# Attention in a fused kernel: other key chunks, v pooled on GpSimd, and another order at the start

## The chip, the cores and the metric

The kernel runs on one core of a Trainium2 chip. The metric is the device time of one execution in microseconds (us). The kernel before takes 1388.67 us as the median of three runs (1388.42 to 1390.24).

## The reference

Three parts run one after the other: attention with pooled keys and values, a mixture of experts with one expert per token, and a feed-forward layer. Only the first is touched:

```python
# q, k, v: (8 batches, 8 heads, 576, 64), float32
k_p = k.reshape(B, H, 72, 8, D).mean(axis=3)      # 72 pooled keys per head
v_p = v.reshape(B, H, 72, 8, D).mean(axis=3)
scores = scale * np.matmul(q, k_p.transpose(0, 1, 3, 2))
scores = scores - np.max(scores, axis=-1, keepdims=True)
attn = np.exp(scores)
attn = attn / (np.sum(attn, axis=-1, keepdims=True) + 1e-09)
return np.matmul(attn, v_p)
# then: logits = x @ w_gate + modality_bias[modality_id]; each token goes to its best expert
```

## The kernel before, in words

Attention runs over 36 tiles of 128 tokens, nine for each pair of batches. One batch has 8 heads of 72 pooled keys, 576 in all. They are held as five chunks of 128 rows: `load_kv` brings eight positions of each row, and `pool_kv` adds them up in three steps (4, 2, 1) into `kvq`, k in the left half and v in the right. Of chunks 0 to 3 each spans two heads, from rows 0, 160, 288 and 448; chunk 4 gathers 32 rows of 128 to 159 and 96 rows of 416 to 511.

A batch is prepared by `prep` or `kv_t` (three transposes by TensorE for each half `z` of the heads, six in all; the keys go scaled into `bd`, the values into `vT`) and by `prep2` (products of v with the gate weights, `pw`; GpSimd multiplies v by masks `mk` into `vb`, so that a chunk has a column block for each head in it, zero outside that head).

A tile goes through six stages. `stage_q` transposes q (four), `stage_s` multiplies with `bd` and takes the maximum on VectorE, `stage_x0` and `stage_e` are the exponentials on ScalarE, `stage_t` transposes `e` (five) and ScalarE copies `eT`, and `stage_a` multiplies `eT` with `vb` into `u` (the attention output, its gate logits and the row sum, 73 columns per head). VectorE and ScalarE (`stage_x`) divide by the row sum, four heads each. Scores of tiles 0 and 1 of a batch (half of the heads each) are both needed for `e` of either.

The order on TensorE, VectorE, ScalarE and SyncE's queue is the order of the code; on GpSimd the scheduler sets it. In pass `i` of the loop the code runs `stage_t(i)`, `stage_e(i+2)`, `stage_x`, `stage_q(i+4)`, `stage_s(i+3)`, what the tables `sched` have for that tile, and `stage_a(i)`. VectorE also gets routing operations between its own (`run_fill`). In front of the loop the first tiles are written out by hand. A PSUM pool `ps_s` has three banks, and `ps_t`, `ps_q` and each half of `u` one.

## Time and profile before

| | us |
|---|---|
| median of three runs | 1388.67 |
| profiled execution | 1387.1 |
| its span in the profile | 1385.3 |
| PE busy | 1357.2 (98%) |
| VectorE busy | 929.2 (67%) |
| ScalarE busy | 641.8 (46%) |
| GpSimd busy | 157.1 (11%) |
| attention's last product with v starts | 179.00 |

Times in the profile count from the start of the span. TensorE has two rows: PEld loads weights, PE multiplies, and loads overlap products. A product on float32 shows two loads and two products in the profile (x12 for six products), a transpose one. The time from the first load of one group to the first load of the next is what the group took on TensorE, waits included.

### The profile page before, as it was taken

Reading aid. Unit: us, or ns where it says so; the run is one execution under the profiler, and the core shown is the slowest. Engines: PE = TensorE matmul, PEld = TensorE weight load, DVE = VectorE, ACT = ScalarE, POOL = GpSimd, SP = SyncE. Lnnn points to the kernel's source line nnn. Section 1 sums busy time; section 2 is a strip of 40 time slices with the busy share of each in tenths; the row PEclk is TensorE's granted clock in tenths of the full one; section 3 lists DMA queues with packets and bytes.
Section 4 is the critical chain, followed back from the end, with each engine's and each line's share of the span. In section 5 each row is a group of like instructions: output and inputs, shape, how many; then the busy total and the mean of one; then the engine's idle time right before and its main releaser. Section 6 shows DMA issues by size and latency. Waiting matters only on the chain.

```text
span 1385.3 us, 24324 instructions
## 1 busy us (share of the span) xinstructions
PE 1357.2 (98%) x7658; PEld 1257.9 (91%) x7658; DVE 929.2 (67%) x1883; ACT 641.8 (46%) x1403; POOL 157.1 (11%) x188
## 2 busy tenths in 40 slices
PE   7999999999999999999999999999999999999998
PEld 5888889999999999999888888888889888888987
DVE  6988776888888888887786445644644564565443
ACT  4888854554455545454444324433433342343322
POOL 3243331111101111100001000100000010001001
PEclk9999999999999999999999999999999999999999
DMA  9996367878778777766645544644454455445441
GB/s 282 291 315 205 119 204 227 262 240 247 238 239 244 239 218 219 218 215 204 193 136 154 167 121 115 178 149 119 123 177 145 116 161 164 115 122 161 120 115 69
DMA packets 229815, 254.41 MB, mean 184 GB/s; under 512 B 19288, under 2 KB 191868, under 8 KB 229724
## 3 DMA queue, kind: packets, MB, share of 16 engines
q1 hardware_dynamic: 223964, 233.16, 56.8%
q0 software_dynamic: 5760, 20.10, 4.0%
q8 instruction: 50, 0.82, 0.3%
q14 instruction: 41, 0.34, 0.1%
HBM read 206.74 MB, written 46.47 MB: 183 GB/s over the span
## 4 chain that ended last, share of the span: by engine, by line
issue 56%; PE 3%; POOL 2%; DVE 1%; DMA 0%; ACT 0%; POOLq 0%; DVEq 0%; ACTq 0%
POOL out_dram L1108 2%; PE ph L943 2%; PE y L956 1%; DVE wl L786 0%; DMA ws<-in_moe_w_dram 0%; ACT wh L785 0%; DVE lo L948 0%; PE pt L871 0%; POOLq L1356 0%; DVE dm L799 0%; DVE da L797 0%; DVE wo L809 0%; ACT hi L947 0%; POOLq L1108 0%; DVE dex L798 0%
## 5 line engine op out<-in xcount | busy, mean ns | idle before, releaser
L1129 PE MATMUL hps<-yc,sq 128*128 128x384 f32 x2004 | 404.3, 336 | 0.6
L1129 PEld LDWEIGHTS hps<-yc,sq 128*128 128x128 f32 x2004 | 358.6, 188 | 32.7 <-ACT s L1170 2.6
L1119 PE MATMUL ops<-wo,gh 128*128 128x512 f32 x1152 | 358.5, 392 | 0.0
L1119 PEld LDWEIGHTS ops<-wo,gh 128*128 128x128 f32 x1152 | 211.4, 188 | 23.1
L1119 PE MATMUL ops<-wo,gl 128*128 128x512 f32 x576 | 228.7, 397 | 0.0
L1141 ACT ACTIVATE r<-c,three 128x384 f32<-128x384 f32 x144 | 88.9, 617 | 205.8 <-DVE c L1151 205.4
L1145 ACT CAST gh<-r 128x384 fp32r<-128x384 f32 x192 | 98.6, 514 | 130.0 <-DVE r L1142 128.6
L786 DVE TENSOR_TENSOR wl<-ws,wh 128x512 fp32r<-128x512 f32 x192 | 129.5, 711 | 15.2 <-ACT wh L785 14.5
L785 ACT CAST wh<-ws 128x512 fp32r<-128x512 f32 x192 | 113.3, 620 | 53.5 <-DMA ws<-in_moe_w_dram 42.1
L956 PE MATMUL y<-hi,wh 128*128 128x400 f32 x384 | 135.0, 351 | 0.5 <-ACT hi L947 0.5
L956 PE MATMUL y<-lo,wh 128*128 128x400 f32 x384 | 132.6, 345 | 1.3 <-DVE lo L948 1.1
L943 PE MATMUL ph<-xhi,wh 128*128 128x400 f32 x384 | 131.9, 344 | 1.0 <-PEq L1356 0.8
L943 PE MATMUL ph<-xlo,wh 128*128 128x400 f32 x384 | 132.7, 345 | 0.0
L943 PE MATMUL ph<-xhi,wl 128*128 128x400 f32 x384 | 132.6, 345 | 0.0
L956 PE MATMUL y<-hi,wl 128*128 128x400 f32 x384 | 131.5, 342 | 0.0
L1119 PEld LDWEIGHTS ops<-wo,gl 128*128 128x128 f32 x576 | 107.9, 187 | 23.1
L1146 DVE TENSOR_TENSOR gl<-r,gh 128x384 fp32r<-128x384 f32 x192 | 106.5, 555 | 31.7 <-ACT gh L1145 27.0
L1108 POOL DMA_INDIRECT out_dram<-osb,tki x36 | 35.3, 979 | 771.9 <-ACT osb L1106 740.7
L1142 DVE SCALAR_TENSOR_TENSOR r<-r,c 128x384 f32<-128x384 f32 x144 | 80.3, 558 | 54.5 <-ACT r L1141 52.4
L863 POOL TENSOR_TENSOR cxg<-cxg 100x512 f32<-100x512 f32 x48 | 57.2, 1194 | 335.6 <-PE ph L943 206.2
L1142 DVE SCALAR_TENSOR_TENSOR r<-r,hps 128x384 f32<-128x384 f32 x48 | 26.6, 554 | 98.3 <-ACT r L1141 98.2
L1141 ACT ACTIVATE r<-hps,three 128x384 f32<-128x384 f32 x48 | 27.9, 582 | 132.1 <-PE hps L1129 132.0
(222 smaller groups left out, 1907.0 us busy)
## 6 DMA issues: line engine op xcount, KB each, us to landing
sq<-sd SPq DMA_DIRECT2D x336, 256.0 KB
ws<-in_moe_w_dram SPq DMA_DIRECT2D x192, 256.0 KB, 3.8
sd<-wq SPq DMA_DIRECT2D x16, 896.0 KB
cxg<-xr SPq DMA_DIRECT2D x44, 225.8 KB
yr<-yd SPq DMA_DIRECT2D x12, 768.0 KB
cs<-in_moe_w_in_dram SPq DMA_DIRECT2D x34, 256.0 KB, 3.7
kv<-in_k_dram SPq DMA_DIRECT2D x16, 512.0 KB
kv<-in_v_dram SPq DMA_DIRECT2D x16, 512.0 KB
```

Of the source, the lines that this page charges most:

```text
L785: nc.scalar.copy(hi, src)
L786: nc.vector.tensor_tensor(lo, src, hi.bitcast(F32), op=ALU.subtract)
L863: nc.gpsimd.tensor_tensor(s.xg[:, t, 0:DM].rearrange("p (h x) -> p h x", x=D), v, s.xg[:, t, GC:GC + 1].unsqueeze(2).to_broadcast([T4, H, ...
L943: nc.tensor.matmul(ph, a[j][:, 0, k * P:(k + 1) * P], b[k], start=(n == 0), stop=(n == 11))
L956: nc.tensor.matmul(yps[d], a[j][:, 1, d * P:(d + 1) * P], b, start=(f == 0 and n == 0), stop=(f == 7 and n == 2))
L1108: i_ = nc.gpsimd.indirect_dma_start(out=out, out_offset=bass.IndirectOffsetOnAxis(ap=tki[:, c:c + 1], axis=0), in_=o, in_offset=None).ins
L1119: nc.tensor.matmul(pso[t_], gt[a][:, t * P:(t + 1) * P], wo[f][:, b], start=(q == 0 and fh == th and n == 0), stop=(q == NQ - 1 and fh != ...
L1129: nc.tensor.matmul(ps, w[:, kk, a * P:(a + 1) * P], y[:, b, kk], start=(start and n == 0), stop=(n == 5), skip_group_check=True)
L1141: a_.activation(r, c, AF.Relu, bias=g.three)
L1142: v.scalar_tensor_tensor(r, r, 6.0, c, op0=ALU.min, op1=ALU.mult)
L1145: a_.copy(gh, r)
L1146: late.append(lambda: v.tensor_tensor(gl, r, gh.bitcast(F32), op=ALU.subtract))
```

## The change

The chunks are five plain runs of 128 rows, from rows 0, 256, 360, 448 and 128 (`KS`), so heads are split into 5 and 3 (`ZH`). Chunk 4 covers three heads, the others two (`HD`). `prep` makes three transposes for the first half and two for the second. `stage_a` opens each half with a product over all of its heads (chunk 4 into five heads, chunk 2 into three; `vb` has zero column blocks for that) and adds the others. `prep2` multiplies by the gate weights in three products that contract over 128 rows instead of six over 64. `stage_e` is one activation instead of two.

GpSimd (`p_`) pools v of batches 0 and 1; VectorE (`v_`) did so before. At the start the tiles go 0, 1, 2 instead of 0, 2, 1; `stage_t(1)` moves in front of the transposes of v of batch 0; and k of batch 1 is pooled behind `prep2(0)`.

```diff
-KR = (0, 160, 288, 448)
+KS = (0, 256, 360, 448, 128)
+HD = ((0, 2), (3, 2), (5, 2), (6, 2), (1, 3))
+VB = (5, 7, 9, 12, 1)
+NB = 14
+ZC = ((4, 0, 1), (2, 3))
+ZH = ((0, 5), (5, 3))
...
-                rows = bass.AP(tensor=src.tensor, offset=src.offset + 288 * z * x, ap=[[x, P], [160 * x, 2], [1, x]])
+                rows = bass.AP(tensor=src.tensor, offset=src.offset + KS[2 * z] * x, ap=[[x, P], [(KS[2 * z + 1] - KS[2 * z]) * x, 2], [1, x]])
                 nc.sync.dma_start(t[:, 2 * z:2 * z + 2], rows)
             else:
-                nc.sync.dma_start(t[0:32, 4], src[128:160])
-                nc.sync.dma_start(t[32:128, 4], src[416:512])
+                nc.sync.dma_start(t[:, 4], src[KS[4]:KS[4] + P])
...
+    def kv_tz(b, d1, ps, z):
+        for c in ZC[z]:
+            o = KS[c] - KS[2 * z]
+            nc.tensor.transpose(ps[0:d1, o:o + P], kvq[b][:, c, 0:d1], g.idn)
...
+    def put_k(b, ps, z, e0):
+        h, n = ZH[z]
+        k8 = ps[0:64, 0:SP * n].rearrange("p (h k) -> p h k", k=SP)
+        if e0:
+            nc.vector.tensor_scalar(bd[b % 3][64:128, h:h + n, SP:2 * SP], k8, KSC, None, op0=ALU.mult)
+        else:
+            nc.scalar.activation(bd[b % 3][64:128, h:h + n, SP:2 * SP], k8, AF.Copy, scale=KSC)
+        nc.scalar.activation(bd[b % 3][0:64, h:h + n, 0:SP], k8, AF.Copy, scale=KSC)
+
+    def put_v(b, ps, z):
+        if z == 0:
+            nc.scalar.copy(vTs[b % 2][0:64, 0:3 * P], ps[64:128, 0:3 * P])
+        else:
+            a = ps[64:128, 0:P]
+            a = bass.AP(tensor=a.tensor, offset=a.offset, ap=[a.ap[0], [KS[3] - KS[2], 2], [1, P]])
+            nc.scalar.copy(vTs[b % 2][64:128, 0:2 * P].rearrange("p (c x) -> p c x", c=2), a)
...
         pw = ps_s.tile([P, 512], F32, name="pw", tag="s")
-        v3 = vT.rearrange("p (z x) -> p z x", z=2)
-        for c in range(4):
-            nc.tensor.matmul(pw[:, 64 * c:64 * c + 64], vT[64:128, KR[c]:KR[c] + P], wg[64:128, :], start=True, stop=True)
-        for z in range(2):
-            nc.tensor.matmul(pw[32 * z:32 * z + 32, 256:320], v3[64:128, z, P:160], wg[64:128, :], start=True, stop=True)
+        two = lambda t, o, d, n: bass.AP(tensor=t.tensor, offset=t.offset + o * E, ap=[t.ap[0], [d * E, 2], [1, n * E]])
+        nc.tensor.matmul(two(pw, 1, 9, 4), vT[:, P:2 * P], two(wg, 1, 3, 4), start=True, stop=True)
+        nc.tensor.matmul(two(pw, 5, 4, 3), vT[:, 0:P], two(wg, 0, 5, 3), start=True, stop=True)
+        nc.tensor.matmul(pw[:, 7 * E:9 * E], vT[:, 2 * P:3 * P], wg[:, 3 * E:5 * E], start=True, stop=True)
...
         t = vb[b % 3]
...
+        for c, o, n, d in ((0, 5, 2, 2), (2, 9, 2, 3), (4, 1, 3, 0)):
+            m = 1 if c == 4 else 2
+            tv = bass.AP(tensor=t.tensor, offset=t.offset + o * UX, ap=[t.ap[0], [d * UX, m], [UX, n], [1, D]])
+            tm = bass.AP(tensor=mk.tensor, offset=mk.offset + o, ap=[mk.ap[0], [d, m], [1, n]])
+            sh = [P, m, n, D]
+            nc.gpsimd.tensor_tensor(tv, x[:, c:c + m, D:2 * D].unsqueeze(2).to_broadcast(sh), tm.unsqueeze(3).to_broadcast(sh), op=ALU.mult)
+        nc.vector.tensor_tensor(t[:, 1:NB, D:XE], pw[:, E:NB * E].rearrange("p (j e) -> p j e", e=E),
+                                mk[:, 1:NB].unsqueeze(2).to_broadcast([P, NB - 1, E]), op=ALU.mult)
...
         if t < 4:
-            h = t % 2
-            i4 = bass.AP(tensor=d.tensor, offset=d.offset, ap=[d.ap[0], [144, 2], [88, 2], [1, 56]])
-            nc.scalar.activation(e[:, :, 136 + 256 * h:248 + 256 * h].rearrange("p a (c x) -> p a c x", c=2), i4, AF.Exp)
-            nc.scalar.activation(e[:, :, 32 * h:32 * h + 32], d[:, 0].rearrange("p (a x) -> p a x", a=2)[:, :, 56:88], AF.Exp)
+            c = 4 * SP * (t % 2) + SP
+            nc.scalar.activation(e[:, :, c:c + 2 * SP], d[:, 0].rearrange("p (t x) -> p t x", t=2), AF.Exp)
         else:
-            i4 = bass.AP(tensor=d.tensor, offset=d.offset, ap=[d.ap[0], [288, 2], [160, 2], [1, P]])
-            nc.scalar.activation(e[:, 0, 64:].rearrange("p (a c x) -> p a c x", a=2, c=2), i4, AF.Exp)
-            nc.scalar.activation(e[:, 0, 0:64].rearrange("p (a x) -> p a x", a=2), d[:, :, P:160], AF.Exp)
+            nc.scalar.activation(e[:, 0], d.rearrange("p x k -> p (x k)"), AF.Exp)
...
-            c0 = 64 + c * P if c < 4 else 0
-            nc.tensor.transpose(ps[:, c * P:(c + 1) * P], e[:, c0:c0 + P], g.idn)
...
         for z in range(2):
-            for n, (c, j, h) in enumerate(((2 * z, 4 * z, 0), (2 * z + 1, 4 * z + 2, 2), (4, 8 + 2 * z, 1))):
+            for n, c in enumerate(ZC[z]):
+                h, m = HD[c] if n else ZH[z]
+                h -= ZH[z][0]
+                v0 = VB[c] - (c == 4)
                 for b, p0, p1 in halves(i):
-                    nc.tensor.matmul(u[z][p0:p1, h:h + 2].rearrange("p j x -> p (j x)"), o[:, c, p0:p1],
-                                     vb[b % 3][:, j:j + 2].rearrange("p j x -> p (j x)"), start=n == 0, stop=n == 2)
+                    nc.tensor.matmul(u[z][p0:p1, h:h + m].rearrange("p j x -> p (j x)"), o[:, c, p0:p1],
+                                     vb[b % 3][:, v0:v0 + m].rearrange("p j x -> p (j x)"), start=n == 0, stop=n == len(ZC[z]) - 1)
...
         x, u, rs = xo.pop(0)
         for c in range(4):
-            nc.scalar.activation(x[:, 4 + c], u[:, c, 0:XE], AF.Copy, scale=rs[:, 4 + c:5 + c])
+            nc.scalar.activation(x[:, 4 + c], u[1][:, c - 1, 0:XE] if c else u[0][:, 4, 0:XE], AF.Copy, scale=rs[:, 4 + c:5 + c])
...
+    for c0, c1_ in ((0, 2), (4, 5), (2, 4)):
+        pool_kv(0, 1, p_, c0, c1_)
     pool_kv(0, 0, v_, 0, 2)
     pool_kv(0, 0, v_, 4, 5)
     ps = kv_ps()
     kv_t(0, D, ps, (0,))
-    put_k(0, ps, (0,))
+    put_k(0, ps[:, 0:512], 0, True)
     stage_q(0)
     pool_kv(0, 0, v_, 2, 4)
     stage_s(0)
     stage_x0(0)
+    kv_t(0, D, ps, (1,))
+    put_k(0, ps[:, 512:1024], 1, True)
+    stage_q(1)
+    stage_s(1)
+    stage_x0(1)
     stage_q(2)
-    kv_t(0, D, ps, (1,))
-    put_k(0, ps, (1,))
+    stage_e(0)
+    stage_e(1)
     stage_s(2)
     stage_x0(2)
-    stage_q(1)
-    pool_kv(0, 1, v_, 0, 2)
-    pool_kv(0, 1, v_, 4, 5)
-    pool_kv(0, 1, v_, 2, 4)
-    stage_s(1)
-    stage_x0(1)
-    stage_e(0)
-    prep_v(0)
-    stage_e(1)
     stage_q(3)
-    pool_kv(1, 0, v_, 0, 2)
-    pool_kv(1, 0, v_, 4, 5)
-    pool_kv(1, 0, v_, 2, 4)
-    prep2(0)
-    at2(1, lambda: pool_kv(1, 1, v_, rs=(2, 1)))
+    for c0, c1_ in ((0, 2), (4, 5), (2, 4)):
+        pool_kv(1, 1, p_, c0, c1_)
     at2(3, bias_all)
     at2(1, lambda: unit_consts(tc, g, c1))
...
-        stage_t(i)
-        stage_e(i + 2)
+        if i != 1:
+            stage_t(i)
+            stage_e(i + 2)
...
+        if i == 0:
+            stage_t(1)
+            stage_e(3)
+            for z in range(2):
+                prep(0, z, "v")
+            prep2(0)
+            for c0, c1_ in ((0, 2), (4, 5), (2, 4)):
+                pool_kv(1, 0, v_, c0, c1_)
         for fn_ in sched2.get(i, ()):
             fn_()
         fill.extend(route_b())
         stage_a(i)
         if i == 0:
-            pool_kv(1, 1, v_, rs=(4,))
             for z in range(2):
                 prep(1, z, "k")
             stage_q(4)
```

On TensorE, from the transposes of v of batch 0 on (`kvps`), through the first transposes of e (`tps`) to the second product with v (`ups`; `qps` are the transposes of q, `sps` the scores), the kernel before has:

```order
L179 MATMUL kvps<-idn,kvq 128x128 x6
L250 MATMUL qps<-idn,q 128x128 x4
L222 MATMUL pw<-wg,vT 128x64 x4
L224 MATMUL pw<-wg,vT 32x64 x2
L323 MATMUL tps<-idn,e 128x128 x5
L280 MATMUL sps<-bd_133,qT 128x144 x4
L344 MATMUL ups<-vb_130,eT 128x146 x6
L204 MATMUL kvps<-idn,kvq 64x128 x6
```

and the kernel after, over the same stretch, from the transposes of q of tile 3:

```order
L255 MATMUL qps<-idn,q 128x128 x4
L323 MATMUL tps<-idn,e 128x128 x5
L285 MATMUL sps<-bd_136,qT 128x144 x4
L323 MATMUL tps<-idn,e 128x128 x5
L191 MATMUL kvps<-idn,kvq 128x128 x5
L230 MATMUL pw<-wg,vT_139 128x2x32
L231 MATMUL pw<-wg,vT_139 128x2x24
L232 MATMUL pw<-wg,vT_139 128x16
L347 MATMUL ups<-vb_133,eT 128x365
L347 MATMUL ups<-vb_133,eT 128x146 x2
L347 MATMUL ups<-vb_133,eT 128x219
L347 MATMUL ups<-vb_133,eT 128x146
```

Both first transposes of e now stand in front of the transposes of v, and a tile's product with v has 1022 columns in five products where it had 876 in six.

On VectorE, from the pooling of v of batch 0 (`kvq<-kv`) on to the gate products of batch 0, the kernel before has (`kv` rows are the first two steps of a pooling):

```order
L173 TENSOR_TENSOR kvq<-kv 128x2x64
L286 TENSOR_REDUCE mx<-sps 128x4 x2
L291 TENSOR_TENSOR d<-sps,mx 128x2x2x72
L173 TENSOR_TENSOR kv<-kv 128x2x256
L173 TENSOR_TENSOR kv<-kv 128x2x128
L173 TENSOR_TENSOR kvq<-kv 128x2x64
L173 TENSOR_TENSOR kv<-kv 128x256
L173 TENSOR_TENSOR kv<-kv 128x128
L173 TENSOR_TENSOR kvq<-kv 128x64
L173 TENSOR_TENSOR kv<-kv 128x2x256
L173 TENSOR_TENSOR kv<-kv 128x2x128
L173 TENSOR_TENSOR kvq<-kv 128x2x64
```

and the kernel after, from the scores of tile 3 to the first row sums (`rs`):

```order
L291 TENSOR_REDUCE mx<-sps 128x4 x2
L296 TENSOR_TENSOR d<-sps,mx 128x2x2x72
L240 TENSOR_TENSOR vb_133<-pw,mk 128x13x8
L186 TENSOR_TENSOR kv<-kv 128x2x256
L186 TENSOR_TENSOR kv<-kv 128x2x128
L186 TENSOR_TENSOR kvq<-kv 128x2x64
L186 TENSOR_TENSOR kv<-kv 128x256
L186 TENSOR_TENSOR kv<-kv 128x128
L186 TENSOR_TENSOR kvq<-kv 128x64
L186 TENSOR_TENSOR kv<-kv 128x2x256
L186 TENSOR_TENSOR kv<-kv 128x2x128
L186 TENSOR_TENSOR kvq<-kv 128x2x64
```

The nine pooling operations that VectorE keeps at the start are those of k of batch 1, and they stand behind the gate products of batch 0 (`vb<-pw`), where before they stood in front of them.

## Rows read from the trace of the kernel before

**Rows 1.** Page: busy time by engine; a group of the last stage (busy, mean | idle).
```profile
PE 1357.2 (98%) x7658; PEld 1257.9 (91%) x7658; DVE 929.2 (67%) x1883; ACT 641.8 (46%) x1403; POOL 157.1 (11%) x188
...
L1119 PE MATMUL ops<-wo,gh 128*128 128x512 f32 x1152 | 358.5, 392 | 0.0
```

**Rows 2.** Timeline of PEld, end of attention: start, us, line, out<-in, count.
```profile
179.00 1.55 PEld L344 LDWEIGHTS ups<-vb,eT 128*128 128x128 f32 x12
```

**Rows 3.** Windows: busy of PE, PEld, DVE, ACT, POOL; PEclk, DMA share, GB/s.
```profile
10.00:20.00 10.00, 7.28 (x43) 6.05 (x42) 7.76 (x19) 3.48 (x12) 1.90 (x5) 0.83 1.07 331
20.00:30.00 10.00, 8.24 (x56) 7.59 (x54) 7.66 (x21) 6.55 (x21) 0.62 (x1) 0.83 0.98 247
110.00:120.00 10.00, 10.00 (x84) 9.53 (x84) 8.39 (x23) 8.82 (x32) 5.46 (x5) 1.00 1.06 295
120.00:130.00 10.00, 8.43 (x95) 7.75 (x94) 9.30 (x36) 8.69 (x27) 1.61 (x2) 1.00 0.44 160
```

**Rows 4.** Timeline of PEld, 149 to 156 us.
```profile
149.11 0.37 PEld L204 LDWEIGHTS kvps<-idn,kvq 128*128 128x128 f32 x3
149.45 1.55 PEld L344 LDWEIGHTS ups<-vb,eT 128*128 128x128 f32 x12
150.93 0.59 PEld L323 LDWEIGHTS tps<-idn,e 128*128 128x128 f32 x5
...
153.11 0.96 PEld L222 LDWEIGHTS pw<-wg,vT 64*128 64x128 f32 x8
154.14 0.14 PEld L224 LDWEIGHTS pw<-wg,vT 64*32 64x32 f32 x4
154.37 1.54 PEld L344 LDWEIGHTS ups<-vb,eT 128*128 128x128 f32 x12
```

**Rows 5.** Timeline of PEld, two waits; in brackets the wait and its releaser.
```profile
47.00 1.54 PEld L344 LDWEIGHTS ups<-vb,eT 128*128 128x128 f32 x12 [1.48 <-issue]
...
145.52 0.10 PEld L428 LDWEIGHTS <-tri 128*128 128x128 bf16 x1 [1.48 <-DVE d L291]
```

**Rows 6.** Timeline of PEld, first and third scores.
```profile
9.66 1.57 PEld L280 LDWEIGHTS sps<-bd,qT 128*128 128x128 f32 x8 [1.33 <-ACT qT L252]
...
16.05 1.03 PEld L280 LDWEIGHTS sps<-bd,qT 128*128 128x128 f32 x8 [1.33 <-ACT qT L252]
```

**Rows 7.** Timeline, start of attention, VectorE.
```profile
15.43 1.14 DVE L173 TENSOR_TENSOR kv<-kv 128x512 f32<-128x512 f32 x2
...
20.64 1.14 DVE L173 TENSOR_TENSOR kv<-kv 128x512 f32<-128x512 f32 x2
...
24.12 0.29 DVE L173 TENSOR_TENSOR kvq<-kv 128x128 f32<-128x128 f32 x1
```

**Rows 8.** Timeline of PEld from the fourth scores to those of batch 1.
```profile
23.76 1.99 PEld L280 LDWEIGHTS sps<-bd,qT 128*128 128x128 f32 x8
25.65 2.29 PEld L344 LDWEIGHTS ups<-vb,eT 128*128 128x128 f32 x12
...
30.70 0.42 PEld L250 LDWEIGHTS qps<-idn,q 128*128 128x128 f32 x4 [1.14 <-ACT qT L252]
31.09 1.04 PEld L280 LDWEIGHTS sps<-bd,qT 128*128 128x128 f32 x8
```

**Rows 9.** What the pooling on VectorE (line 173) waited for: us, times.
```profile
  DMA kv<-in_k_dram: 3.5, 1
```

**Rows 10.** Timeline of VectorE and GpSimd, both on two SBUF inputs, 42 to 50 us.
```profile
42.25 0.68 POOL L492 TENSOR_TENSOR t<-mf,bb 128x288 f32<-128x288 f32 x1
...
42.36 1.25 DVE L173 TENSOR_TENSOR kv<-kv 128x640 f32<-128x640 f32 x1
43.00 1.26 POOL L493 TENSOR_TENSOR bia<-bia,t 128x288 f32<-128x288 f32 x1
...
48.09 0.81 DVE L173 TENSOR_TENSOR kv<-kv 128x640 f32<-128x640 f32 x1
...
49.51 1.04 POOL L229 TENSOR_TENSOR vb<-kvq,mk 128x512 f32<-128x512 f32 x1 [5.24 <-DVE rs L352]
```

More of the change, by code (lines that the diff above doesn't have):

```diff
@@ L100, in attention @@
     nc.vector.memset(zb, 0.0)
[L101 to L102 removed]
+    wg = c1.tile([P, H * E], F32, name="wg")
+    nc.vector.memset(wg, 0.0)
+    mk = c1.tile([P, NB], F32, name="mk")
     nc.gpsimd.memset(mk, 1.0)
[L104 to L111 removed]
+    for n in (0, 4, 11):
+        nc.gpsimd.memset(mk[:, n:n + 1], 0.0)
+    for n in range(5):
+        for r in range(HD[n][1]):
+            m = mk[:, VB[n] + r:VB[n] + r + 1]
+            h = HD[n][0] + r
+            lo, hi = max(SP * h - KS[n], 0, 40 if n == 3 else 0), min(SP * (h + 1) - KS[n], P)
+            if lo > 0:
+                nc.gpsimd.affine_select(m, m, pattern=[[0, 1]], compare_op=ALU.is_ge, fill=0.0, base=-lo, channel_multiplier=1)
+            if hi < P:
+                nc.gpsimd.affine_select(m, m, pattern=[[0, 1]], compare_op=ALU.is_ge, fill=0.0, base=hi - 1, channel_multiplier=-1)
+    vb = [c1.tile([P, NB, UX], F32, name=f"vb{i}") for i in range(3)]
     bd = [c1.tile([P, H, 2 * SP], F32, name=f"bd{i}") for i in range(3)]
+    vTs = [c1.tile([P, 3 * P], F32, name=f"vT{i}") for i in range(2)]
     nc.gpsimd.memset(bd[0], 0.0)
+    for i in range(2):
+        nc.gpsimd.memset(vTs[i][64:128, 2 * P:3 * P], 0.0)
     for i in range(3):
[L115 removed]
+        for n in (0, 4, 11):
+            nc.gpsimd.memset(vb[i][:, n, 0:XE], 0.0)
         nc.scalar.activation(vb[i][:, :, XE:UX], mk.unsqueeze(2), AF.Copy, scale=float(POOL))
@@ L203, in prep @@
-        for c, o in ((4, P - 32 * z), (2 * z, 0), (2 * z + 1, 160)):
-            nc.tensor.transpose(ps[0:d1, o:o + P], kvq[b][:, c, 0:d1], g.idn)
+        kv_tz(b, 2 * D if "v" in which else D, ps, z)
         if "k" in which:
-            k8 = ps[0:64, 0:288].rearrange("p (h k) -> p h k", k=SP)
-            nc.scalar.activation(bd[b % 3][64:128, 4 * z:4 * z + 4, SP:2 * SP], k8, AF.Copy, scale=KSC)
-            nc.scalar.activation(bd[b % 3][0:64, 4 * z:4 * z + 4, 0:SP], k8, AF.Copy, scale=KSC)
+            put_k(b, ps, z, False)
@@ L350, in stage_a @@
         rs = p3.tile([P, H], F32, name="rs", tag="rs")
-        for z in range(2):
-            nc.vector.tensor_scalar(rs[:, 4 * z:4 * z + 4], u[z][:, :, XE], POOL * 1e-9, None, op0=ALU.add)
+        for z, (h, m) in enumerate(ZH):
+            nc.vector.tensor_scalar(rs[:, h:h + m], u[z][:, :, XE], POOL * 1e-9, None, op0=ALU.add)
             run_fill()
@@ L517, in attention @@
     load_kv(0, 1, (0, 2, 1))
-    nc.sync.dma_start(wg[64:128].rearrange("p (h e) -> p h e", e=E), wgh)
+    for z, (h, n) in enumerate(ZH):
+        nc.sync.dma_start(wg[64 * z:64 * z + 64, E * h:E * (h + n)].rearrange("p (h e) -> p h e", e=E), wgh[:, h:h + n])
     load_kv(1, 0, (0, 2, 1))
```

58 lines of the change are left out of this document (9 added, 49 removed).

## The prediction

> **What bounds the kernel now.** I read the page first: PE is busy for 98% of the span, VectorE for 67%, and in the last stage PE stands idle for 0.0 us before the products of the costliest groups [rows 1]. Nothing of that stage is changed, so it passes on whatever attention gains or loses. The timeline of the weight loads shows where attention ends: its last product with v starts at 179.00 [rows 2], and the first expert's products follow without a pause. What counts is therefore how much later or earlier that moment comes. (PE stands for TensorE, z for one half of the heads, k1 for k of batch 1.)
>
> Next the windows, by stage. At 110 to 120 us PE is busy for 10.00 of 10 us and VectorE for 8.39; at 120 to 130 it is 8.43 against 9.30 [rows 3]. So PE sets the pace most of the time, and in between there are stretches in which it waits for VectorE. The loads' timeline shows such waits one by one: 1.48 us at 47.00 ("issue", behind VectorE's and ScalarE's work on the previous output), and 1.48 us at 145.52 for VectorE's `d` [rows 5]. In the first 30 us no engine is full: PE has 7.28 and 8.24 of 10, at a mean granted clock of 0.83, and VectorE 7.76 and 7.66 [rows 3]. There it is a chain from engine to engine.
>
> **The change part by part.**
>
> *Product with v.* From 149.45 to 150.93 one tile's six products, 876 columns, took 1.48 us on PE [rows 4], 1.69 ns per column. They now have 365 + 146 + 146 + 219 + 146 = 1022 columns, 146 more, so 0.247 us more. The transposes beside them need 0.11 us each, so weight loads of this shape keep pace with the columns, and one load fewer gives nothing. Over 36 tiles: +8.9 us of PE time. Below this nothing speaks for a gain, except that the loads were the limit after all: five products for six would then give 1.48/6 = 0.25 us less per tile.
>
> *Transposes of k and v.* Three took 149.45 - 149.11 = 0.34 us [rows 4]; one of six goes, 0.11 us for each of 8 batches: -0.9 us.
>
> *Gate products.* Eight loads of 128 columns took 154.14 - 153.11 = 1.03 us, 0.129 each, though a product has only 64 columns; with the four small ones it is 1.26 us [rows 4]. Now there are three products, six loads: 6 x 0.129 = 0.77 us. That is -0.49 us a batch, -3.9 us in all. If the wider contraction made loads slower it would be less; were columns the limit (128 instead of 384), up to -0.8 us a batch.
>
> Together PE has 8.9 - 0.9 - 3.9 = +4.1 us more. Not all of it lies on the path: a wait for VectorE takes up what was added since the last one. Going through the loads from 45 to 170 us, from the wait at 47.00 to the one at 145.52 and two smaller ones behind it [rows 5], I find about 12 tiles out of 29 with a wait over 0.4 us. I take 40% of growth and savings alike as covered: 0.6 x 4.1 = +2.4 us. The ends are 0 (all covered) and +4.1 (none).
>
> *Exponentials, masks, row sums.* One activation instead of two, one VectorE operation instead of two per batch, and the first head of ScalarE's four now comes from the other half of `u`. ScalarE is busy for 8.82 and 8.69 of 10 us [rows 3], VectorE was treated above; I cost this at nothing. What hides it is PE's own time. Without that cover it could give back some 0.1 us a tile in the waiting tiles, 1 us, or cost as much, since the first product of a tile now waits for ScalarE's first output too, where only the second half did.
>
> *The start.* Scores of the first and the third tile start at 9.66 and 16.05 [rows 6], 3.2 us a tile, before the pooling of v (from 15.43 [rows 7]) gets in the way. At this pace the fourth comes at 19 to 20 instead of 23.76 [rows 8]. But before the first product with v PE now also has the second tile's transposes, and ScalarE the copies behind them: about 1.2 us for the fourth scores, then some 3 us on ScalarE (four exponentials, `eT`, `e`, two `vT`), then gate products and masks, 1 us. The product comes at about 25.4, against 25.65 [rows 8]: no gain there by itself.
>
> Then the pooling of k1 decides. Before, VectorE did it from 20.64 to 24.41 [rows 7], 3.77 us, in the shadow of other work; the scores of batch 1 followed at 31.09 [rows 8]. Now it stands behind `vb<-pw` in VectorE's order, so it starts at about 25.4 and ends at 29.2 at the earliest. Behind it wait the two last transposes of k1 (0.3), two copies into `bd` (0.8), `qT` (0.6), the next transposes of q, which wait for `qT` as at 30.70 [rows 8] (0.4), and then the scores: 31.5, so +0.4 us. Row sums and the first outputs are queued behind the pooling on VectorE, and ScalarE's outputs wait for them, but they are due only after those scores.
>
> *v on GpSimd.* VectorE is rid of some 4 us for each of two batches. But GpSimd works at the same time as that pooling. k0, q0, v0, k1 and q1 (6.0 MB) lie in front of v1 in the queue; at 331 GB/s [rows 3] v1 arrives from 21 or 22 us on. A GpSimd operation on 512 columns takes 1.04 us [rows 10]; scaled to the smaller steps, v1 needs about 5.4 us, and 1.7 us more for the masks, till 29. The trace shows what two such operations do to each other: on 640 columns VectorE needs 0.81 us alone and 1.25 beside GpSimd, which needs 0.68 alone and 1.26 beside VectorE [rows 10]. With 0.44/0.81 = 54% on three quarters of the 3.77 us (the rest are gaps between dependent steps) the pooling of k1 takes 1.5 us longer. The start: 0.4 + 1.5 = +1.9 us. The ends: -1.5 us, if the fourth scores come at 19 and ScalarE is quicker than I add up, and +2.9 us, if every step waits for GpSimd. Pooling of v0 is done by about 19, before PE comes to it at 22. SyncE's queue issues one DMA less per load; the loads of batches 2 and 3 wait for buffers that are pooled some 7 us later than before. That is hidden as long as pooling doesn't wait for data: it did so once, 3.5 us at the very start [rows 9].
>
> [...]
>
> **Sum.** +2.4 (tiles) + 1.9 (start) = +4.3 us. Against its own time the profiled execution of 1387.1 us becomes 1391.4; the median of the runs is 1388.67, 1.6 us above it, so 1393.0.
>
> **The rivals.**
>
> *Covered (no change).* ScalarE and VectorE, at 8.4 to 9.3 of 10 us [rows 3], are near enough to full that they set the tile's pace and PE's growth disappears in its waits; the start comes out even. For it: the waits in [rows 5]. Against it: 10.00 of 10 us of PE at 110 to 120 [rows 3], and a load timeline without gaps from 149.45 to 150.93 [rows 4]. It gives 0 to +2 us, 1389.7.
>
> *Faster.* The start is what the edit gives: the fourth scores move from 23.8 to 19 and VectorE loses the pooling of v. If the first product with v starts 3 us earlier, at 22.5, and GpSimd is through with its steps on v1 by then (or they hardly meet), batch 1's scores come at 28.5, 2.6 us earlier. With nearly all of PE's growth covered, and 1 us from ScalarE's single exponential, that is -3.5 us: 1385.2. It decides if those scores start before 28. Against it: ScalarE's list of seven operations behind the fourth scores.
>
> *More than the sum.* All of the growth on the path (+4.1), every step of k1's pooling behind GpSimd (+2.9), and a low clock after it: after the waits of the first 20 us PE's mean clock fell to 0.83 [rows 3], and the first product with v took 2.29 us instead of 1.55 [rows 8, 4]. A second idle time from 27 to 33 us could bring this once more, +1.5 us: +8.5, 1397.2.
>
> **How the numbers follow.** Forecast 0.55, covered 0.20, faster 0.10, more 0.15. The range of 8 in 10 goes from 1386.5, which cuts off most of the faster case, to 1397.0. A difference under 0.2% (2.8 us) can't be told from none in such a kernel. Of the forecast's 0.55 I give 0.08 to an outcome under +2.8; with the covered case "same" is 0.28, "faster" 0.10, and "slower" 0.47 + 0.15 = 0.62.
>
> **What would show it.** In the new profile one tile's product with v should take 1.7 us between loads, the gate products 0.75 to 0.8 us, and pooling steps of k1 on VectorE should be drawn out beside GpSimd's on v1, with batch 1's first scores at 32 to 34 us. The last product with v should start at 182 to 185 instead of 179.00. I am wrong if the product with v doesn't grow, if those scores come before 30, or if the waits at `d` shrink by as much as the products grow.

## The result, and the profile after

The changed kernel takes 1397.78 us (median of 6 runs, 1396.10 to 1398.84), the kernel before on the same occasion 1388.60 (6 runs, 1387.76 to 1390.24): a ratio of 1.0064, 95% interval 1.0053 to 1.0075. That is 9.2 us slower. The forecast had 4.3 us and a range up to 1397.0, so the direction was right and the size wrong.

TensorE's busy time on the page of the profile after, which answers to [rows 1], grew by 4.5 us:

```profile
PE 1361.7 (98%) x7520; PEld 1254.9 (90%) x7520; DVE 925.9 (66%) x1864; ACT 638.8 (46%) x1368; POOL 168.0 (12%) x224
```

Where the time went is read from three moments on the loads' timeline: the third tile's transposes of `e` (the end of the start), the last product with v, and the first expert product.

| profiled execution | third tile's transposes | last product with v | first expert product |
|---|---|---|---|
| before | 33.55 | 179.00 | 180.68 |
| after | 39.67 | 187.74 | 189.67 |
| difference | +6.1 | +8.7 | +9.0 |

So the start cost 6.1 us, the tiles 2.6, and the passage into the experts 0.3. (The spans of these two executions differ by 10.5 us, 1395.8 against 1385.3; the other 1.5 lie behind the first expert product, where nothing was changed.) These are the rows of after for the second and the third column, which answer to [rows 2]:

```profile
187.74 1.79 PEld L347 LDWEIGHTS ups<-vb,eT 128*128 128x128 f32 x10
...
189.67 0.19 PEld L950 LDWEIGHTS ph<-xhi,wh 128*128 128x128 f32 x1
```

The windows show the start. They answer to [rows 3], with 30 to 40 us added (PE, PEld, DVE, ACT, POOL; PEclk, DMA share, GB/s):

```profile
10.00:20.00 10.00, 7.19 (x46) 6.37 (x46) 4.49 (x10) 5.91 (x20) 8.62 (x21) 0.88 1.08 365
20.00:30.00 10.00, 6.04 (x35) 4.68 (x33) 6.62 (x11) 3.06 (x9) 8.71 (x13) 0.80 0.88 227
30.00:40.00 10.00, 8.08 (x32) 6.78 (x31) 3.61 (x11) 4.60 (x14) 1.11 (x2) 0.51 1.06 380
110.00:120.00 10.00, 9.28 (x76) 8.57 (x74) 8.17 (x26) 9.07 (x29) 2.00 (x2) 1.00 0.84 252
```

GpSimd is now busy for 8.6 and 8.7 of 10 us, VectorE is relieved from 10 to 20 us, and from 30 to 40 us PE has a mean granted clock of 0.51, and 0.50 in each window of 2 us from 28 to 38. The timeline of the weight loads shows how it got there; it answers to [rows 8]:

```profile
21.83 0.20 PEld L191 LDWEIGHTS kvps<-idn,kvq 128*128 128x128 f32 x2 [0.50 <-issue]
23.63 0.30 PEld L230 LDWEIGHTS pw<-wg,vT 128*128 128x128 f32 x2 [1.60 <-ACT vT L215]
...
24.90 2.33 PEld L347 LDWEIGHTS ups<-vb,eT 128*128 128x128 f32 x10 [0.53 <-DVE vb L240]
29.44 0.40 PEld L191 LDWEIGHTS kvps<-idn,kvq 128*64 128x64 f32 x3 [2.21 <-issue]
31.45 0.18 PEld L191 LDWEIGHTS kvps<-idn,kvq 128*64 128x64 f32 x2 [1.62 <-issue]
31.67 0.87 PEld L255 LDWEIGHTS qps<-idn,q 128*128 128x128 f32 x4
33.67 0.72 PEld L255 LDWEIGHTS qps<-idn,q 128*128 128x128 f32 x4 [1.13 <-ACT qT L257]
34.37 1.99 PEld L285 LDWEIGHTS sps<-bd,qT 128*128 128x128 f32 x8
36.27 0.58 PEld L347 LDWEIGHTS ups<-vb,eT 128*128 128x128 f32 x2
...
39.67 0.63 PEld L323 LDWEIGHTS tps<-idn,e 128*128 128x128 f32 x5
```

The first product with v comes at 24.90, 0.75 us earlier than before. While it runs, at about 26, the clock falls: the window from 24 to 28 us has a mean of 0.76, the one from 30 to 40 above 0.51. (The higher clock is 1.00, as from 110 to 120 us, the lower one 0.50.) Before that PE had waited 0.50, 1.60 and 0.53 us with work in between. At the lower clock it then waits 2.21 and 1.62 us for k1, the scores of batch 1 come at 34.37 instead of 31.09, and still at the lower clock they take 36.27 - 34.37 = 1.90 us and the product with v behind them 39.67 - 36.27 = 3.40 us; at the higher clock these are 0.97 and 1.72 (rows of a later tile below). This is the first of these windows:

```profile
24.00:28.00 4.00, 3.16 (x15) 2.42 (x14) 3.35 (x5) 0.00 (x0) 3.84 (x5) 0.76 0.57 144
```

What PE waited for is on VectorE, which answers to [rows 7]:

```profile
24.77 2.11 DVE L186 TENSOR_TENSOR kv<-kv 128x512 f32<-128x512 f32 x2
26.91 0.70 DVE L186 TENSOR_TENSOR kvq<-kv 128x128 f32<-128x128 f32 x1
...
30.86 0.48 DVE L186 TENSOR_TENSOR kvq<-kv 128x128 f32<-128x128 f32 x1
```

and beside it on GpSimd:

```profile
24.87 3.32 POOL L186 TENSOR_TENSOR kv<-kv 128x512 f32<-128x512 f32 x3
...
29.78 0.76 POOL L186 TENSOR_TENSOR kvq<-kv 128x64 f32<-128x64 f32 x1
```

The pooling of k1 runs from 24.77 to 31.34, 6.57 us instead of 3.77; its first two steps took 2.11 us, where before they took 1.14 [rows 7]. GpSimd's pooling of v1, and its masks, lie beside it all the while.

The steady state, where one tile follows the other, answers to [rows 4]:

```profile
156.78 0.26 PEld L191 LDWEIGHTS kvps<-idn,kvq 128*128 128x128 f32 x2
157.05 1.78 PEld L347 LDWEIGHTS ups<-vb,eT 128*128 128x128 f32 x10
158.77 0.59 PEld L323 LDWEIGHTS tps<-idn,e 128*128 128x128 f32 x5
159.33 0.47 PEld L255 LDWEIGHTS qps<-idn,q 128*128 128x128 f32 x4
159.77 1.04 PEld L285 LDWEIGHTS sps<-bd,qT 128*128 128x128 f32 x8
160.74 0.31 PEld L230 LDWEIGHTS pw<-wg,vT 128*128 128x128 f32 x2
160.97 0.30 PEld L231 LDWEIGHTS pw<-wg,vT 128*128 128x128 f32 x2
161.19 0.30 PEld L232 LDWEIGHTS pw<-wg,vT 128*128 128x128 f32 x2
161.42 1.79 PEld L347 LDWEIGHTS ups<-vb,eT 128*128 128x128 f32 x10
```

A product with v takes 158.77 - 157.05 = 1.72 us (forecast 1.7), the gate products 161.42 - 160.74 = 0.68 (forecast 0.77), scores 0.97.

### The profile page after: what moved, and what is told of

Its sections match the earlier page's. It is cut to its first block, busy times and chain, and to the rows that moved or that the text cites. A ratio compares the mean times of both kernels' runs of the same rounds, so it can differ in the third digit from the quotient of the medians.

```text
span 1395.8 us, 24016 instructions
## 1 busy us (share of the span) xinstructions
PE 1361.7 (98%) x7520; PEld 1254.9 (90%) x7520; DVE 925.9 (66%) x1864; ACT 638.8 (46%) x1368; POOL 168.0 (12%) x224
## 4 chain that ended last, share of the span: by engine, by line
issue 56%; PE 2%; POOL 2%; DVE 1%; DMA 0%; ACT 0%; POOLq 0%; SPq 0%; DVEq 0%; ACTq 0%
POOL out_dram L1115 2%; PE y L963 1%; PE ph L950 1%; DMA ws<-in_moe_w_dram 0%; DVE wl L793 0%; DVE lo L955 0%; ACT wh L792 0%; PE pt L878 0%; DVE wo L816 0%; POOLq L1363 0%; DVE dex L815 0%; ACT dex L801 0%; DVE da L804 0%; DVE dm L806 0%; DVE yo L907 0%
## 5 line engine op out<-in xcount | busy, mean ns | idle before, releaser
L1126 PEld LDWEIGHTS ops<-wo,gh 128*128 128x128 f32 x1152 | 211.4, 188 | 23.1
L1126 PEld LDWEIGHTS ops<-wo,gl 128*128 128x128 f32 x576 | 107.9, 187 | 23.1
```

The costliest lines, as they stand in the source:

```text
L1126: nc.tensor.matmul(pso[t_], gt[a][:, t * P:(t + 1) * P], wo[f][:, b], start=(q == 0 and fh == th and n == 0), stop=(q == NQ - 1 and fh != ...
```

## The experiments

The kernels were timed on four occasions, each beside the kernel before (ratio to it with 95% interval). On the first three the kernel before itself took 1400.6 to 1401.0 us, on the fourth 1388.3. The expectations of the first occasion (`e1` to `e4`) name times as if it took 1388.6; they are read as differences from that.

### The parts apart

**Chunks alone** (`e4_chunks`): the changed kernel with the start of before.

```diff
-    for c0, c1_ in ((0, 2), (4, 5), (2, 4)):
-        pool_kv(0, 1, p_, c0, c1_)
     pool_kv(0, 0, v_, 0, 2)
...
+    pool_kv(0, 1, v_, 0, 2)      # and 4:5, 2:4; tiles 0, 2, 1 again
...
-        if i != 1:
-            stage_t(i)
-            stage_e(i + 2)
+        stage_t(i)
+        stage_e(i + 2)
```

> The new chunks alone: the kernel after with the start of the kernel before (v pooled by VectorE, tiles 0, 2, 1, k of batch 1 pooled in front of the gate products). Theory (start): only the tiles' part is left, 2.0 us between the third and the last tiles and 0.9 at the end: 1390.5 to 1392. Rival (columns): 1395 to 1397.

Measured: 1.0039 (1.0025 to 1.0053), +5.4 us, more than expected. In its trace the third tile's transposes come at 35.30, so 1.75 us were lost at the start even in the old order, where TensorE was slow from 23.1 to 28 us at least, by its loads (its scores at 25.29 took 1.90 us, at the higher clock 0.97; in before the clock was 0.50 from 23.7 to 27.2); the rest, some 3.6 us, agrees with the tiles' +2.6 within the interval (3.5 to 7.4 for the whole).

**Start alone** (`e5_start`): the kernel before with the new start.

```diff
+    for c0, c1_ in ((0, 2), (4, 5), (2, 4)):
+        pool_kv(0, 1, p_, c0, c1_)
...
+        pool_kv(1, 1, p_, c0, c1_)
...
+        if i == 0:
+            stage_t(1)
+            stage_e(3)
...
+                pool_kv(1, 0, v_, c0, c1_)
```

> The start of the changed kernel (GpSimd adds up v of both batches, e's transposes of tile 1 ahead of those of v) on the old chunks. Theory (the start carries two thirds: 6.1 us at the first tile's transposes, from the shared additions of k and v and from the low clock behind them): 4.5 to 6.5 us above the kernel before, k1's additions on VectorE 6 to 7 us long, the clock at 0.50 for some 10 us, an AV stage still 1.48 us. Rival (the chunks carry it, and the start's delay is made up in waits later): at most 3 us above.

Measured: 1.0026 (1.0015 to 1.0038), +3.6 us, between the two. The transposes come at 38.90, 5.4 us later than before, so part of the delay may be made up later; where stays open, since the pauses told of in the last section lie between. The pooling of k1 took 6.26 us in its trace, beside GpSimd. The two parts, 5.4 + 3.6 = 9.0 us, make up the whole, each of them good to about 2 us.

**The changed kernel again**, on the second and the third occasion (`c_after`, `g_after`).

> The changed kernel itself again, beside the three runs below on one chip. Theory (start and columns, nothing of the chip): 1.0064 times the kernel before, its last transposes of the first tile near 39.7 us and the first expert product 9 us later than in the kernel before. Rival (some of the +9.2 was that chip's own): a ratio under 1.005. It also shows whether the common pauses of 1.9 to 2.1 us of all engines after 100 us, which the first four kernels showed and neither the kernel before nor the changed one did, belong to the chip (then they are here too) or to those kernels (then they are not).

> The changed kernel once more, so that the next run is compared with it on one and the same chip. Both theories: 1.006 times the kernel before.

Measured: 1.0060 (1.0047 to 1.0074) and 1.0058 (1.0046 to 1.0070). Transposes at 40.09 and 39.20, so the end of the start in a single trace is good to about half a microsecond. The slow stretches vary more: in `c_after` the scores at 9.70 and 34.88 took 1.84 and 1.90 us (0.97 at the higher clock), and the loads of the product with v at 25.26 took 2.43 instead of 1.79, much as in after; in `g_after` the granted clock is 0.50 only from 31.3, behind a wait of 2.82 us, to 38.2, though the scores at 10.04 took 1.85 us there too, in windows that have it at 1.00.

### What makes the start late

**k1 earlier** (`e1_k1_first`): pooling of k1 on VectorE ahead of `vb<-pw`.

```diff
     stage_q(3)
+    pool_kv(1, 0, v_, 0, 2)
...
             stage_e(3)
+            pool_kv(1, 0, v_, 4, 5)
+            pool_kv(1, 0, v_, 2, 4)
...
-            for c0, c1_ in ((0, 2), (4, 5), (2, 4)):
-                pool_kv(1, 0, v_, c0, c1_)
```

> The kernel after, with the pooling of k of batch 1 moved in VectorE's order in front of the gate products of batch 0 (its first chunks in front of the fourth tile's maximum). Theory (start): of the 9.2 us lost, 6.1 arise before the second tile's output, because this pooling stands behind the gate products, runs beside GpSimd and leaves PE idle until its clock is low. Then batch 1's first scores come at 31 to 32 us instead of 34.4, at the full clock, and the time is 1391.5 to 1393.5. Rival (columns): the wider products with v cost nearly all of it and the start is made up for later; then 1397 to 1398.

Measured: 1.0063 (1.0050 to 1.0075); nothing gained. The steps met GpSimd all the same, only earlier, and now stood in front of `vb`: one of them took 1.25 us (0.29 in before), and `vb` came at 29.05 instead of 24.58. Some 2.4 us of that, by the author's estimate, are a slow TensorE: the first three scores took 1.84 to 1.85 us each here, 0.97 at the higher clock (so they did in the next run, whose `vb` came at 27.00); some 2 us are left for the steps. VectorE's timeline of this run:

```profile
22.24 1.25 DVE L186 TENSOR_TENSOR kvq<-kv 128x128 f32<-128x128 f32 x1
...
29.05 0.26 DVE L240 TENSOR_TENSOR vb<-pw,mk 128x104 f32<-128x104 f32 x1
```

**v1 on VectorE** (`e2_v1_vector`):

```diff
-    for c0, c1_ in ((0, 2), (4, 5), (2, 4)):
-        pool_kv(1, 1, p_, c0, c1_)
+    at2(1, lambda: pool_kv(1, 1, v_, rs=(2, 1)))
...
         if i == 0:
+            pool_kv(1, 1, v_, rs=(4,))
```

> The kernel after, but v of batch 1 is pooled by VectorE, at the places of the kernel before; GpSimd pools only v of batch 0. Theory (start, by contention): the pooling of k of batch 1 takes 3.8 us instead of 6.6, batch 1's scores come at about 31.6, and the time is 1392.5 to 1395; VectorE has 2.8 us of pooling more, which its pauses hide. Rival (place alone): the pooling's place behind the gate products is what costs, beside GpSimd or not: 1396.5 to 1398. Rival (columns): 1397 to 1398.5.

The contention is gone, as its timeline of VectorE shows: 27.18 to 30.95, 3.77 us again, and 1.14 for the steps that took 2.11 in after.

```profile
27.18 1.14 DVE L186 TENSOR_TENSOR kv<-kv 128x512 f32<-128x512 f32 x2
28.35 0.29 DVE L186 TENSOR_TENSOR kvq<-kv 128x128 f32<-128x128 f32 x1
...
29.48 1.14 DVE L186 TENSOR_TENSOR kv<-kv 128x512 f32<-128x512 f32 x2
30.66 0.29 DVE L186 TENSOR_TENSOR kvq<-kv 128x128 f32<-128x128 f32 x1
```

```profile
35.83 0.59 PEld L323 LDWEIGHTS tps<-idn,e 128*128 128x128 f32 x5
```

The transposes come at 35.83, 4.88 us behind the end of the pooling (after: 8.33). But in this trace PE was slow up to nearly 22 us (the first three scores in 1.84 to 1.85 us each instead of 0.97, the last of them from 17.99), all of it came 2.4 us later (first product with v at 27.32, in after at 24.90), and the time hardly moved: 1.0052 (1.0036 to 1.0068).

**Clock in the late gaps** (`e3_warm`): ten products of zeros where PE waits for k1.

```diff
+            idle = ps_q.tile([P, 512], F32, name="wps", tag="q")
             for z in range(2):
+                for _ in range(4 - z):
+                    nc.tensor.matmul(idle, zb[:, 0:P], zb[:, 0:512], start=True, stop=True)
                 prep(1, z, "k")
             stage_q(4)
+            # and three more into a tile of ps_t
```

> The kernel after, with ten products of zeros that nobody reads in PE's idle time between the first product with v and batch 1's scores (four, three and three). Theory (clock): the low clock from 26 to 39.6 us costs some 3 us on the scores and the second product with v; with PE busy the clock is back before the scores, the second product with v takes 1.7 instead of 3.4 us, and the time is 1394.5 to 1396. Without a cost of the clock: 1397.5 to 1399, since the products of zeros only add work.

```profile
36.38 0.59 PEld L323 LDWEIGHTS tps<-idn,e 128*128 128x128 f32 x5
```

From 14 us on every scores group up to the third tile's transposes takes 0.96 or 0.97 us, as at the higher clock. The pooling of k1 still takes some 6.55 us beside GpSimd and ends at about 31.50, estimated from the loads on either side of it (the product with v at 25.09, the last transposes of k1 at 31.62; in after 24.90 and 31.45), but the transposes of `e` come at 36.38, again some 4.9 us behind it and 3.3 us earlier than in after; the time again doesn't show it, 1.0063 (1.0050 to 1.0075). The two single edits left open whether the start reaches the end at all.

**Both** (`e11_start_eased`): the edits of the two runs above together.

> The changed kernel, with both terms of its start that were sized too small taken away: VectorE adds up v of batch 1 as before (no shared additions of k1 and v1), and ten products of zeros stand in TensorE's gaps of the start (its clock has no idle time to fall in). Theory (these two are the 4 us by which the start exceeded the forecast, and they reach the end): the first tile's transposes near 35 us instead of 40, and 3.5 to 5 us less than the changed kernel in the same call. Rival (what the start gains is lost again in waits later, as the ends of the two single edits suggest, 7.5 and 8.2 us above the kernel before): within 1 us of the changed kernel.

Measured: 1.0035 (1.0023 to 1.0047) against 1.0058 (1.0046 to 1.0070) for the changed kernel on the same occasion, 1406.39 against 1408.97: 2.6 us less, good to about 2, and short of the 3.5 expected. Transposes at 37.52, not 35: again at the lower clock (0.50) from 8 to 21.6 us, and once more from 28.4 to 31.8.

**Clock in all gaps** (`e13_start_full`): the same, with products of zeros in the early gaps too, into the bank of `u` that is not in use yet (`warm(n)` issues n of them).

```diff
-    for _ in range(WU):
+    for _ in range(WU + 6):
...
+    warm(6)
     stage_s(0)
...
+    warm(6)
     stage_s(1)
...
+    warm(5)
     stage_s(2)
```

> The changed kernel with its start eased altogether: batch 1's v on VectorE as before, and products of zeros in every gap of TensorE up to the third tile (before the first scores too, where the run with products in the late gaps alone still fell to 0.50). Theory (contention and the clock are all by which the start was late beyond its place): clock 1.00 from 6 us on, third tile's transposes at 33.5 to 35 us, and what is left over the kernel before is the growth of the products with v: 2 to 3.5 us. Rival (the start does not reach the end, or something else in it is late): transposes after 36, or 5 us and more over the kernel before.

Windows of this run, and the end of the start on the loads' timeline:

```profile
8.00:24.00 16.00, 12.40 (x90) 9.83 (x88) 7.77 (x17) 9.89 (x30) 10.85 (x32) 1.00 1.11 350
24.00:28.00 4.00, 3.66 (x12) 2.88 (x13) 3.77 (x12) 0.00 (x0) 0.00 (x0) 0.59 0.20 18
28.00:40.00 12.00, 11.74 (x92) 9.75 (x92) 9.12 (x22) 8.83 (x28) 1.65 (x3) 1.00 1.05 376
```

```profile
31.63 1.04 PEld L285 LDWEIGHTS sps<-bd,qT 128*128 128x128 f32 x8
32.59 1.80 PEld L347 LDWEIGHTS ups<-vb,eT 128*128 128x128 f32 x10
34.33 0.59 PEld L323 LDWEIGHTS tps<-idn,e 128*128 128x128 f32 x5
```

The start is as expected: transposes at 34.33, 0.8 us behind the kernel before, scores of batch 1 at 31.63, a clock of 1.00 from 8 to 40 us outside of 23.9 to 27.3. In that stretch the product with v runs slowly (27.49 - 24.34 = 3.15 us instead of 1.72), and the transposes of k1 behind them come at 28.26 and 29.24, though VectorE was done with k1 at 27.98. The first expert product comes at 184.60, 3.9 us behind the kernel before and 5.1 ahead of after, whose start ended 5.3 us later: on this occasion, without the pauses, practically all that the start gained reaches the experts. The time is 1.0034 (1.0021 to 1.0047), +4.7 us: more than the 2 to 3.5 expected, less than the rival's 5, though the interval (2.9 to 6.5) holds part of either.

**Clock in the kernel before** (`e14_before_warm`): the same products in the gaps of before, nothing else.

```diff
+    warm(6)
     stage_s(0)
...
+    warm(10)
     prep2(0)
```

> The kernel before, with products of zeros in TensorE's gaps of its start and nothing else. Theory (a low clock in the start costs time at the end, in the kernel before too): clock 1.00 over 8 to 28 us instead of 0.50 in two stretches, third tile's transposes at 31.5 to 32.5 instead of 33.3, 1 to 2 us below the kernel before. Rival (VectorE's additions of k and v pace the start, TensorE's speed is beside them): transposes within 0.4 us of 33.3, time within 0.7 us.

```profile
8.00:24.00 16.00, 13.83 (x108) 11.24 (x106) 14.00 (x35) 8.13 (x25) 4.63 (x18) 1.00 1.07 338
24.00:28.00 4.00, 3.31 (x28) 3.06 (x27) 2.65 (x8) 3.09 (x11) 0.00 (x0) 1.00 0.81 110
```

Those are its windows: the clock doesn't fall there. The third tile's transposes start at 31.06 instead of 33.55, the first expert product at 178.38 instead of 180.68, and the time is 0.9978 (0.9969 to 0.9987), 3 us below the kernel before. So the low clock in its start did cost time at the end.

This also bounds what the clock explains of the change. With products of zeros in both kernels, and the contention gone from the changed one, it stands at 1.0034 and the kernel before at 0.9978, on one occasion: some 8 us apart, good to 2; the starts end at 34.33 and 31.06, the first expert products come at 184.60 and 178.38. So most of the 9.2 us is still there with the gaps of both kernels filled.

### The tiles

**Columns** (`e7_narrow`): zero blocks narrower, 949 columns for 1022.

```diff
-VB = (5, 7, 9, 12, 1)
-NB = 14
-ZC = ((4, 0, 1), (2, 3))
+VB = (3, 6, 8, 11, 0)
+NB = 13
+ZC = ((0, 1, 4), (2, 3))
```

> The changed kernel with its opening products narrow: chunk 0 opens heads 0 to 2 with one block of zeros and chunk 2 heads 5 to 7, chunk 4 comes last, so that an AV stage has 949 columns instead of 1022. Nothing else moves. Theory (columns set the time of an AV stage, 0.247 us of growth for what the change added, about 6 tenths of it on the path): an AV stage 0.12 us shorter than in the changed kernel, 36 of them, 2.5 us off the time (up to 4.4 if all of it is on the path). Rival (the stage is bound by its waits, not by its columns): stage shorter, time within 0.7 us of the changed kernel.

Measured: 1405.51 against 1407.86, 2.35 us less, good to about 2. Its product with v takes 1.60 us, 0.12 less than in after, as 73 columns at 1.69 ns say; 36 x 0.12 = 4.3, of which roughly half reached the end.

**Head 4 on VectorE** (`e6_head4`):

```diff
-        nc.vector.tensor_tensor(x[:, 0:4], u[0][:, 0:4, 0:XE], rs[:, 0:4]...
+        nc.vector.tensor_tensor(x[:, 0:5], u[0][:, :, 0:XE], rs[:, 0:5]...
...
-        for c in range(4):
-            nc.scalar.activation(x[:, 4 + c], ...
+        for c in range(3):
+            nc.scalar.activation(x[:, 5 + c], ...
```

> The changed kernel, with head 4 divided by VectorE together with heads 0 to 3 (one operation of five heads), ScalarE divides three heads instead of four. Theory (the products with v wait for ScalarE's last division before they may write their two banks again, a wait that the forecast costed at nothing): 1 to 2 us below the changed kernel, the waits behind ACT xg at the products with v fall from 5.6 us to under 2.5. Rival (that wait only stands in for a later one, ScalarE's work was beside the path): within 0.5 us of the changed kernel.

Measured: 1406.60 against 1407.86, 1.3 us less (1404.71 to 1407.09 against 1406.76 to 1409.52, so just about told apart). The idle time of PE's loads before the products with v, 40 to 180 us, first in the changed kernel of the same occasion, then in this run (busy, mean | idle and what ended it):

```profile
L347 PEld LDWEIGHTS ups<-vb,eT 128*128 128x128 f32 (+1 forms) x321 | 44.4, 179 | 18.5 <-ACT xg L368 8.5 <-issue 3.6
```

```profile
L347 PEld LDWEIGHTS ups<-vb,eT 128*128 128x128 f32 (+1 forms) x320 | 45.2, 181 | 16.0 <-issue 5.0 <-ACT eT L325 3.5 <-ACT xg L368 0.4
```

The wait for ScalarE's `xg` is gone, 8.1 us of it, but 5.6 us came back as waits for `eT`, issue and others; 2.5 us are left over, and 1.3 in the time. Both traces have the pauses of the last section in them; in after, without them, the wait for `xg` comes to 3.8 us, and in the kernel before to 1.6.

**Gate products on the old chunks** (`e10_gate`): the kernel before with two chunks per gate product.

```diff
-        for c in range(4):
-            nc.tensor.matmul(pw[:, 64 * c:64 * c + 64], vT[64:128, KR[c]:KR[c] + P], wg[64:128, :], ...
+        for c in range(2):
+            nc.tensor.matmul(two(pw, 2 * c), vT[:, KR[c]:KR[c] + P], two(wg, 2 * c), ...
```

> The kernel before, with nothing of the change but the idea of its gate products: v's transposes of the two halves stand one above the other in 128 rows, so that one product forms the gates of two chunks against a weight that is zero off its two blocks; four products of 32 columns take the place of six of 64. Theory (a product of fewer columns that fills 128 rows is cheaper, and 6 tenths of TensorE's time reach the end): the group falls from 1.26 us to 0.8 to 0.9, eight of them 3 us, 1.5 to 2.5 us below the kernel before. Rival (the gate products stand beside the waits for VectorE's vb): within 0.7 us of it.

Measured: 0.9989 (0.9977 to 1.0000), 0 to 3 us less; the group takes 0.76 us. Where it stands right before a routing product that needs VectorE's `d`, that product now waits up to 1.3 us; behind one such wait, 1.29 us at 63.29, the product with v at 63.44 took 2.85 us instead of 1.48, nearly twice its time, as in the windows of the lower clock.

**Gate and clock** (`e12_gate_warm`): that and the products of zeros.

> The kernel before with the two things that paid: the gate products of two chunks at a time, and products of zeros in the gaps of the start. Theory: the two add, 2.5 to 4 us below the kernel before, below both kernels. Rival (the start is paced by VectorE, and shorter gate products only wait longer for VectorE's vb and d): 1.5 us or less, what the gate products alone gave.

Measured: 0.9980 (0.9967 to 0.9993). It beats both kernels, but not by more than the products of zeros alone. Its loads' timeline shows one place where the saved time turned against it:

```profile
39.70 0.52 PEld L224 LDWEIGHTS pw<-wg,vT 128*128 128x128 f32 x4 [1.65 <-ACT vT L214]
40.26 0.19 PEld L227 LDWEIGHTS pw<-wg,vT 64*32 64x32 f32 x4
40.51 2.93 PEld L346 LDWEIGHTS ups<-vb,eT 128*128 128x128 f32 x12
43.35 0.77 PEld L325 LDWEIGHTS tps<-idn,e 128*128 128x128 f32 x5
```

```profile
40.00:44.00 4.00, 4.00 (x23) 3.88 (x23) 3.72 (x10) 0.00 (x0) 2.82 (x3) 0.57 1.06 367
```

PE waits 1.65 us for `vT`, the clock falls (0.57 in that window), and the product with v takes 2.84 us instead of 1.48.

## Why the prediction was wrong

*Right.* The direction, and the sizes on TensorE: 1.72 us for a product with v (forecast 1.7), 0.68 for the gate products (0.77). The tiles came to +2.6 us between the first two moments of the table, where the forecast had +2.4. Some luck is in that: by the measured sizes PE's growth is 36 x 0.24 - 0.9 - 8 x 0.58 = +3.1 us and not +4.1, a term put at nothing (below) lies in the +2.6 too, and the loads from 45 to 170 us show 10 waits over 0.4 us, not 12.

*The step that failed* is "The start: 0.4 + 1.5 = +1.9 us". It measured 6.1. Two terms of it were mis-sized: the contention, 1.5 us, measured 2.8, and the lower clock behind the waits, which the sum has at nothing, cost 3.3 to 3.5. On the forecast's own path, the pooling of k1 was to end at 29.2 + 1.5 = 30.7 and ended at 31.34; batch 1's scores were to come at 31.5 + 1.5 = 33.0 and came at 34.37; and these scores and the product with v behind them took 5.30 us where the same take 0.97 + 1.72 = 2.69 at the higher clock (1.00). By the end of the start in four traces:

| | third tile's transposes | step |
|---|---|---|
| before | 33.55 | |
| start eased altogether | 34.33 | +0.8: k1's place in VectorE's order, two longer products with v (forecast 0.4, and 0.5 among the tiles), and this run's own low clock |
| clock kept in the late gaps alone | 36.38 | +2.0: pooling of k1 beside GpSimd (forecast 1.5) |
| after | 39.67 | +3.3: low clock (0.50) from 26 to 39.7 us (forecast 0) |

(The third of these was slow early on too, with scores of 1.85 us at 9.49, as after was, which has a clock of 0.50 from 10 to 12 us.) The second row is not clean, as its own stretch at the lower clock held up k1's transposes. The operations themselves give a cleaner split: the pooling of k1 took 6.57 us in after and 3.77 alone, +2.8; from its end to the third tile's transposes it is 8.33 us in after and 4.88 and about 4.9 in the two runs whose scores there take 0.97 us, as at the full clock (`e2_v1_vector`, `e3_warm`), +3.5. Together that is all of the 6.1, and nothing is left for k1's place.

All this is against the kernel before as it stood, which the forecast worked from. That kernel loses 2.5 us in its own start where the clock is low (33.55 against 31.06 with products of zeros), so the last row is not what the clock adds to the difference between two kernels that both keep it up: those still lie some 8 us apart. Of that, 3.3 us are the starts (34.33 against 31.06), and no run takes them apart.

The contention was sized by half overlap: 54% on three quarters of 3.77 us. The quarter taken as gaps between the steps is not in the trace of before: its nine steps fill 3.71 of the 3.77 us. In after seven of the nine were drawn out, by 6.57 - 3.77 = 2.8 us in all. VectorE's first step (from 24.77) took 0.70 us (alone 0.68); GpSimd's operation from 24.87 took 1.72 us, where its like took 1.26 at 15.91; and VectorE's second step, from 25.50, took 1.38 us instead of 0.42 and ended 0.29 us behind that operation. The upper end of the start and the rival "More than the sum" have +2.9 us instead, for every step behind GpSimd. No row or run shows that term; the runs showed seven steps drawn out by 2.8 us beside GpSimd, and 3.77 us again without it (`e2_v1_vector`). Of its two sizes the forecast took the smaller.

The clock was the larger miss. The forecast saw that it had fallen after waits in the kernel before (0.83 from 10 to 20 us), and an idle time from 27 to 33 us that the change would add, but put the effect at 1.5 us into a rival of 0.15. It fell before that idle time, at 26, and stayed low through it until 39.7; scores and a product with v took twice their time. Added up, the rival "More than the sum" (+8.5) was the right story; its terms came out as 2.8 for the contention (forecast there 2.9), 2.6 for the tiles (4.1) and 3.3 for the clock (1.5).

*A term costed at nothing.* ScalarE's share of the first half of `u` cost some 1.3 us by the times. If so, it lies within the +2.6 of the tiles, and of PE's growth of 3.1 only the other 1.3 was on the path, under half.

*What stays open.* By times, the two terms of the start are worth 1.0064 - 1.0034 = 0.30% or, within one occasion, 1.0058 - 1.0035 = 0.23%, that is 3 to 4 us, against 5 to 6 in the traces; each of the two edits alone moved the transposes by over 3 us and the time by nothing that can be told; and the run with the early gaps filled as well (1.0034) is no better by its time than the one without (1.0035), though its start ends 3.2 us earlier in the traces. The traces show one reason why the times are so blunt: behind the first expert product, where all these kernels have the same code, the profiled executions took from 1202.6 to 1210.1 us. The longest of these is the run with both edits, at 1410.4 the slowest of its eight (1402.3 to 1410.4). Why the part behind the experts' start varies is not known.

## What to carry to other kernels

Moving work to an idle engine can be no gain when it then runs beside like work that others wait for: VectorE's pooling took 6.57 us beside GpSimd's and 3.77 without. Price such a pair from rows that show both at once, and not as two queues that run free. Waits on TensorE can cost themselves and then what follows at the lower clock (here 5.30 us for what takes 2.69 at the higher), so a start full of short waits deserves a trial with products of zeros in its gaps: that alone took 3 us from the kernel before, though the changed kernel's times show nothing of it by itself. And wider products that save instructions still cost by their columns: 1.72 us for 1022 in five products, 1.48 for 876 in six.
